# Decoding float64 weights: signs moved to GpSimd, and a third raw buffer

## The chip, the cores and the metric

The program runs on one core of one Trainium2 chip. The metric is the device time of one execution in microseconds (us), from runs on the chip; the median of the runs stands for a kernel. The hardware profiler takes one execution apart: TensorE matmuls (PE), TensorE weight loads (PEld), VectorE (DVE), ScalarE (ACT), GpSimd (POOL) and the DMA queue of SyncE (SP). About 0.2% (1.4 us) is what a measurement of this kernel can tell from no change.

## The reference

The reference is an attention layer followed by a gated feed-forward layer. Attention has 4 batches, 8 heads, 768 positions and a head width of 64; a position sees the first 8 keys and the 95 keys before itself, with a penalty that grows with distance. The feed-forward layer takes 3072 tokens of width 512 through 2048 hidden units:

```python
x = attn_out.transpose(0, 2, 1, 3).reshape(B * S, H * D)
h = x @ w_in
g = h * np.clip(h + 3.0, 0.0, 6.0) / 6.0
return (g @ w_out).astype(np.float32)
```

The two weight matrices are float64 (random numbers divided by the square root of 512 or of 2048), everything else is float32. Nothing on the chip computes in float64 here, so the kernel reads each weight as two 32-bit words and builds a float32 from them.

## The kernel before, in words

**Tiling.** The 3072 tokens form 8 blocks of 384 (`TB`). The hidden width is cut into 16 slices of 128 (index f). For each block and slice TensorE makes `hp = w1[f]^T x` (12 matmuls on line 166), ScalarE and VectorE gate it (lines 177 and 178) and split the result into a high part `gh` (line 184 or 186) and a rest `gl` (line 191), and 9 more matmuls (line 198) add it to the block's output. Each float32 operand is kept as two parts, hi and lo, and three products stand for one.

**Attention** works on pairs of heads, 4 pairs for a block, so pairs 0 to 11 belong to the first three blocks, which are done at the start with nothing else to fill TensorE. For a pair: scores on TensorE (line 816), distances and row minimum on VectorE (line 831), exponentials on ScalarE (line 835), row sums and their reciprocal on VectorE (lines 845, 846; tile `sums`), normalization on GpSimd (line 855, six instructions, tile `n`), transposes on TensorE (lines 863 and 865, tile `tp` or `hp`, copied out on line 867), and the product with the values (line 907, tile `xp`), which goes to the block's `xh` and `xl` (lines 152 and 153).

**Weights.** They come in 32 chunks of 128 x 512 float64; chunk 2f is slice f of w_in, chunk 2f+1 slice f of w_out. Slice f can be used only when its chunks are decoded. Function `fetch` reads a chunk into a raw tile `wst` (line 363). `magnitude` takes the absolute value of the high words on ScalarE (line 371, tile `wz`) and the scaled low words on GpSimd (line 375, tile `we`). For the first 12 chunks (`helped`) GpSimd also clamps `wz` to the range in which the exponent can be moved over (line 378); for the other 20 VectorE does it (line 400). The generator `decode` then runs four steps for a chunk, all on VectorE: mask and shift (line 401); the rest `lo` of the chunk before (line 406); the sign put in from the raw high word (line 409); and the integer sum with the low word (line 415), after which the next chunk's `magnitude` is issued and ScalarE casts `hi` (line 419). The next-but-one chunk is fetched right behind the sign step. There are two tiles each of `wst`, `wz` and `we`.

**Order.** The instructions of TensorE, SyncE's queue and GpSimd are kept in the order in which the program issues them (`in_order`); those of VectorE and ScalarE are placed by a scheduler when the program is built. Where decoding steps fall among attention and matmuls is set by `work`, which adds up stated costs of TensorE and VectorE work and issues steps (each yields its own stated cost) while VectorE's sum is the smaller, up to `allowed`; `decoded_to` issues what a slice must have before it is used. Engines run in order: an instruction that waits holds up all behind it on its engine or queue.

## Time and profile before

| what | value |
|---|---|
| median of 3 runs (lowest, highest) | 676.43 us (676.08, 676.55) |
| span of the profiled execution | 675.4 us |
| TensorE matmuls busy | 658.0 us, 97% |
| VectorE, ScalarE, GpSimd busy | 421.2, 278.5, 230.2 us |
| mean granted TensorE clock | 0.992 |
| decoding, from the first to the last instruction on `wz` | 16.6 to about 169 us |

The span runs from the first to the last instruction. A timeline row has the start, the duration, engine, line, operation, the tiles written and read, and in square brackets how long the engine was idle before it and what released it. A duration contains some 0.06 to 0.1 us in which the next instruction has already begun, so the distance between two starts is the better cost of an instruction that follows another.

### The profile page before, as it was taken

How to read it: one execution, taken by the hardware profiler on the slowest of the kernel's cores; microseconds unless marked ns; L12 is line 12 of the kernel's file. 1: busy time of each engine (PE TensorE's matmuls, PEld its weight loads, DVE VectorE, ACT ScalarE, POOL GpSimd, SP SyncE). 2: the span in 40 equal slices, each digit the busy share in tenths (PEclk: the TensorE clock that was granted, in tenths of full speed). 3: DMA queues.
4: the chain of work that ended last, by engine and by line, in shares of the span. 5: the costliest groups of instructions: out<-in, count | busy, mean ns of one | idle time of the engine just before them, and what ended most of it. 6: DMA issues, size and time to landing. Idle time of an engine off the chain costs nothing.

```text
span 675.4 us, 11454 instructions
## 1 busy us (share of the span) xinstructions
PE 658.0 (97%) x3963; PEld 587.2 (87%) x3963; DVE 421.2 (62%) x1109; ACT 278.5 (41%) x736; POOL 230.2 (34%) x401
## 2 busy tenths in 40 slices
PE   9989599999999999999999999999999999999997
PEld 7769488888999999989998999899898999989995
DVE  6798889999324776557663777547763677422222
ACT  6898555655225433143332444143331434221111
POOL 5778642221001443324341444314531444302110
PEclk9999889999999999999999999999999999999999
DMA  8675444442003267635654266734455255610001
GB/s 290 185 249 183 168 151 154 138 144 94 1 1 113 67 167 195 167 95 139 151 148 125 93 161 175 195 94 117 129 166 152 71 154 142 141 48 2 1 1 52
DMA packets 60836, 84.73 MB, mean 125 GB/s; under 512 B 8416, under 2 KB 45536, under 8 KB 60768
## 3 DMA queue, kind: packets, MB, share of 16 engines
q1 hardware_dynamic: 60480, 83.64, 42.7%
q8 instruction: 33, 0.54, 0.3%
q14 instruction: 35, 0.29, 0.1%
q10 hardware_dynamic: 288, 0.26, 0.1%
HBM read 62.92 MB, written 20.97 MB: 124 GB/s over the span
## 4 chain that ended last, share of the span: by engine, by line
PE 79%; DVE 9%; DMA 5%; ACT 3%; POOL 2%; issue 2%; SPq 0%; POOLq 0%; ACTq 0%; DVEq 0%
PE hp L166 34%; PE acc L198 32%; DMA wst<-w 5%; PE xp L907 2%; PE sp L820 2%; PE tp L907 2%; DVE wz L409 2%; PE tp L820 2%; ACT n L835 2%; DVE wz L415 1%; POOL n L855 1%; PE xp L358 1%; DVE wz L401 1%; DVE n L831 1%; DVE gl L191 1%
## 5 line engine op out<-in xcount | busy, mean ns | idle before, releaser
L177 ACT ACTIVATE g<-hp,small 128x384 f32<-128x384 f32 x127 | 73.7, 580 | 251.6 <-PE hp L166 230.5
L166 PE MATMUL hp<-xh,w1h 128*128 128x384 f32 x512 | 174.0, 340 | 0.0
L166 PE MATMUL hp<-xh,w1l 128*128 128x384 f32 x512 | 172.7, 337 | 0.0
L166 PE MATMUL hp<-xl,w1h 128*128 128x384 f32 x512 | 171.9, 336 | 0.0
L184 POOL TENSOR_SCALAR gh<-g 128x384 fp32r<-128x384 f32 x96 | 51.8, 540 | 292.3 <-DVE g L178 261.7
L198 PE MATMUL acc<-w2h,gl 128*128 128x512 f32 x336 | 133.8, 398 | 0.2
L198 PE MATMUL acc<-w2l,gh 128*128 128x512 f32 x336 | 133.1, 396 | 0.0
L198 PE MATMUL acc<-w2h,gh 128*128 128x512 f32 x336 | 132.9, 395 | 0.0
L178 DVE SCALAR_TENSOR_TENSOR g<-g,hp 128x384 f32<-128x384 f32 x128 | 69.7, 545 | 90.1 <-ACT g L177 89.7
L191 DVE TENSOR_TENSOR gl<-g,gh 128x384 fp32r<-128x384 f32 x128 | 80.6, 630 | 53.2 <-POOL gh L184 44.9
L855 POOL TENSOR_SCALAR n<-n,sums 128x232 f32<-128x232 f32 (+1 forms) x186 | 103.1, 570 | 31.2 <-DVE sums L846 17.6
L835 ACT ACTIVATE n<-n,least 128x232 f32<-128x232 f32 (+1 forms) x192 | 89.3, 468 | 44.0 <-DVE least L831 42.0
L166 PEld LDWEIGHTS hp<-xh,w1h 128*128 128x128 f32 x512 | 96.3, 188 | 5.5 <-issue 1.5
L166 PEld LDWEIGHTS hp<-xl,w1h 128*128 128x128 f32 x512 | 96.2, 188 | 3.9
L166 PEld LDWEIGHTS hp<-xh,w1l 128*128 128x128 f32 x512 | 96.0, 188 | 0.0
L198 PEld LDWEIGHTS acc<-w2h,gl 128*128 128x128 f32 x336 | 63.4, 189 | 15.4 <-DVE gl L191 1.7
L198 PEld LDWEIGHTS acc<-w2h,gh 128*128 128x128 f32 x336 | 63.8, 190 | 10.4 <-POOL gh L184 0.3
L198 PEld LDWEIGHTS acc<-w2l,gh 128*128 128x128 f32 x336 | 63.6, 189 | 10.4
L880 DVE STREAM_TRANSPOSE blocks<-n 128x256 f32<-128x256 f32 x112 | 43.5, 424 | 30.5 <-POOL n L855 17.3
L375 POOL TENSOR_SCALAR we<-wst 128x512 int32<-128x512 uint32 x32 | 26.6, 832 | 64.6 <-DMA wst<-w 56.7
L791 POOL TENSOR_SCALAR kx<-load 64x504 fp32r<-64x504 f32 (+1 forms) x40 | 31.1, 778 | 43.9 <-PE hp L166 42.3
L831 DVE CUSTOM_DVE_ANT_0 n<-sp,d 128x232 f32<-128x232 f32 (+1 forms) x70 | 23.6, 374 | 29.6 <-PE sp L820 29.1
(111 smaller groups left out, 788.3 us busy)
## 6 DMA issues: line engine op xcount, KB each, us to landing
wst<-w SPq DMA_DIRECT2D x32, 512.0 KB, 3.5
load<-pairs SPq DMA_DIRECT2D x22, 636.0 KB, 5.2
there<-blocks SPq DMA_DIRECT2D x52, 256.0 KB, 2.6
load<-pairs SPq DMA_DIRECT2D x32, 384.0 KB, 4.2
weights<-there SPq DMA_DIRECT2D x48, 192.0 KB, 3.9
out<-o SPq DMA_DIRECT2D x23, 256.0 KB, 2.1
weights<-there SPq DMA_DIRECT2D x32, 160.0 KB, 3.2
load<-pairs SPq DMA_DIRECT2D x9, 444.0 KB, 4.2
```

The lines of the kernel that those rows point to most:

```text
L166: self.nc.tensor.matmul(hp, lhsT=self.w1(w, f)[:, kt, :], rhs=a[:, kt, :], start=(n == 0), stop=(n == 3 * NKT - 1))
L177: nc.scalar.activation(out=g, in_=hp, func=AF.Relu, bias=self.three, scale=1.0)
L178: nc.vector.scalar_tensor_tensor(out=g, in0=g, scalar=6.0, in1=hp, op0=ALU.min, op1=ALU.mult)
L184: self.nc.gpsimd.tensor_scalar(out=gh, in0=g, scalar1=1.0, scalar2=0.0, op0=ALU.mult, op1=ALU.add)
L191: self.nc.vector.tensor_tensor(out=gl, in0=g, in1=gh.bitcast(F32), op=ALU.subtract)
L198: self.nc.tensor.matmul(acc[tt], lhsT=a[:, tk], rhs=self.w2(w, f), start=(f == 0 and j == 0), stop=(f == NF - 1 and j == 2))
L791: nc.gpsimd.tensor_scalar(out=part["kx"][own, c], in0=k[own, c], scalar1=1.0, scalar2=0.0, op0=ALU.mult, op1=ALU.add)
L820: nc.tensor.matmul(sp[j][:, lo:W], lhsT=q[:, t], rhs=part["kx"][:, c], start=(m == 0), stop=(m == 1))
L831: nc.vector.tensor_tensor_reduce(out=e[:, j, lo:W], in0=sp[j][:, lo:W], in1=d, op0=ALU.add, op1=ALU.min, scale=scale, scalar=3.0e38, accum ...
L835: nc.scalar.activation(out=e[:, j, lo:W], in_=e[:, j, lo:W], func=AF.Exp, bias=self.least[:, i:i + 1], scale=-1.0, accum_out=self.sums[:, ...
L855: nc.gpsimd.tensor_scalar(out=e[:, j, lo:W], in0=e[:, j, lo:W], scalar1=over, scalar2=0.0, op0=ALU.mult, op1=ALU.add)
L880: nc.vector.transpose(out=blocks[:, :, s].rearrange("p b j q -> p j b q"), in_=e[:, :, c:c + P].rearrange("p j (b q) -> p j b q", b=4))
```

## The change

It removes the sign step on VectorE, so a chunk takes three steps. ScalarE's absolute value now has a scale of 2^-80, VectorE clamps every chunk to limits that are smaller by the same factor, and mask and shift keep one bit more. Behind the low words, GpSimd compares the raw high words with zero and writes 0 or 32768 into the upper halves of the tile `we`, as 16-bit numbers at every second place; the integer sum then brings in low word and sign together. GpSimd's clamp for the first 12 chunks is gone. The raw tiles are three, and chunk i+2 is fetched at the start of chunk i's steps. The stated costs and the limits on steps are those of three steps.

```diff
+WORDS = 3
+DOWN = 2.0 ** -80
@@ magnitude
-        self.nc.scalar.activation(out=self.z[i].bitcast(F32), in_=words[:, :, 1].bitcast(F32), func=AF.Abs)
+        high = words[:, :, 1].bitcast(F32)
+        self.nc.scalar.activation(out=self.z[i].bitcast(F32), in_=high, func=AF.Abs, scale=DOWN)
...
         self.nc.gpsimd.tensor_scalar(out=self.e[i], in0=words[:, :, 0].bitcast(U32), scalar1=2.0 ** -29, scalar2=0.0, op0=ALU.mult, op1=ALU.add)
-        if self.helped(i):
-            z = self.z[i].bitcast(F32)
-            self.nc.gpsimd.tensor_scalar(out=z, in0=z, scalar1=MOST, scalar2=LEAST, op0=ALU.min, op1=ALU.max)
+        signs = self.e[i].bitcast(U16).rearrange("p (c w) -> p c w", w=2)[:, :, 1]
+        self.nc.gpsimd.tensor_scalar(out=signs, in0=high, scalar1=0.0, scalar2=float(1 << 15), op0=ALU.is_lt, op1=ALU.mult)
@@ decode
             if a:
+                if i + 2 < N:
+                    self.fetch(i + 2)
                 z = self.z[i]
-                if not self.helped(i):
-                    ts(out=z.bitcast(F32), in0=z.bitcast(F32), scalar1=LEAST, scalar2=MOST, op0=ALU.max, op1=ALU.min)
-                ts(out=z, in0=z, scalar1=0x07FFFFFF, scalar2=3, op0=ALU.bitwise_and, op1=ALU.logical_shift_left)
-            yield (0.34 if self.helped(i) else 0.68) * a
+                ts(out=z.bitcast(F32), in0=z.bitcast(F32), scalar1=LEAST * DOWN, scalar2=MOST * DOWN, op0=ALU.max, op1=ALU.min)
+                ts(out=z, in0=z, scalar1=0x0FFFFFFF, scalar2=3, op0=ALU.bitwise_and, op1=ALU.logical_shift_left)
+            yield 0.78 * a
...
-            yield 0.6 * b
-            if a:
-                stt(out=z, in0=self.raw[i].rearrange("p (c w) -> p c w", w=2)[:, :, 1], scalar=-0x40000000, in1=z,
-                    op0=ALU.bitwise_and, op1=ALU.bitwise_or)
-                if i + 2 < N:
-                    self.fetch(i + 2)
-            yield 0.6 * a
+            yield 0.64 * b
...
-            yield 0.69 * a
+            yield 0.66 * a
@@ banded
-            self.decoding(words, 2, 2, side="right")
+            self.decoding(words, WORDS, 2, side="right")
...
-            self.allowed = 4 * NF + 3
+            self.allowed = 3 * NF + 2
```

TensorE's order is the same before and after. Three places of the other engines differ in what matters below (line numbers of the changed kernel are some lines off: 379 is the low words, 381 the signs, 401 the clamp, 402 mask and shift, 850 the normalization, 366 the fetch).

GpSimd before, from the normalization of pair 10 (tiles `n` with `sums_871`) to that of pair 11 (`sums_1007`); `we_1121` belongs to chunk 7:

```order
L855 TENSOR_SCALAR n_961<-n_961,sums_871 128x232 x2
L375 TENSOR_SCALAR we_1121<-wst_1039 128x512
L378 TENSOR_SCALAR wz_1120<-wz_1120 128x512
L375 TENSOR_SCALAR we_1153<-wst_1080 128x512
L378 TENSOR_SCALAR wz_1152<-wz_1152 128x512
L375 TENSOR_SCALAR we_1186<-wst_1134 128x512
L378 TENSOR_SCALAR wz_1185<-wz_1185 128x512
L855 TENSOR_SCALAR n_1009<-n_1009,sums_1007 128x128 x2
```

And of the change, from the normalization of pair 9 (`sums_795`) to that of pair 10 (`sums_878`); `we_1002` belongs to chunk 5:

```order
L850 TENSOR_SCALAR n_806<-n_806,sums_795 128x232 x2
L379 TENSOR_SCALAR we_1002<-wst_910 128x512
L381 TENSOR_SCALAR we_1002<-wst_910 128x512
L379 TENSOR_SCALAR we_1043<-wst_953 128x512
L381 TENSOR_SCALAR we_1043<-wst_953 128x512
L379 TENSOR_SCALAR we_1084<-wst_1007 128x512
L381 TENSOR_SCALAR we_1084<-wst_1007 128x512
L850 TENSOR_SCALAR n_880<-n_880,sums_878 128x128 x2
```

Three chunks in a row stand ahead of pair 11 before, and ahead of pair 10 now, with two (chunks 8 and 9) ahead of pair 11. Up to pair 11 the count is the same: chunks 0 to 9, two GpSimd instructions each. From chunk 12 on there is one instruction more for a chunk than before.

SyncE's queue before, around the fetches of chunks 6 to 10 (with what each waits for; names with DMAHW are earlier transfers):

```order
L363 DMA wst_998<-w 128x1024 [waits DVE_49,DMAHW5_49,Activation_49,Pool_49]
L363 DMA wst_1039<-w 128x1024 [waits DMAHW2_49,DVE_49,DMAHW6_49,Activation_49,Pool_49]
L290 DMA load2_167<-pairs 128x768 [waits DMAHW3_49,PE_49]
L363 DMA wst_1080<-w 128x1024 [waits DMAHW1_49,DVE_49,DMAHW4_49,Activation_49,Pool_49]
L363 DMA wst_1134<-w 128x1024 [waits DVE_49,DMAHW2_49,Activation_49,Pool_49]
L363 DMA wst_1168<-w 128x1024 [waits DVE_49,DMAHW4_49,Activation_49,Pool_49]
```

And of the change, around the fetches of chunks 6 to 10:

```order
L366 DMA wst_953<-w 128x1024 [waits Activation_49,Pool_49]
L293 DMA load1_73<-pairs 128x1272 [waits DMAHW1_49,PE_49]
L366 DMA wst_1007<-w 128x1024 [waits DMAHW2_49,DMAHW3_49,Activation_49,Pool_49]
L366 DMA wst_1048<-w 128x1024 [waits DMAHW6_49,Activation_49,Pool_49]
L293 DMA load2_167<-pairs 128x768 [waits DMAHW4_49,PE_49]
L366 DMA wst_1110<-w 128x1024 [waits DMAHW0_49,DMAHW5_49,Activation_49,Pool_49]
L366 DMA wst_1143<-w 128x1024 [waits DMAHW2_49,Activation_49,Pool_49]
```

The fetch no longer waits for VectorE, only for ScalarE and GpSimd to have read the chunk three before. Against the loads of attention data it stands one chunk earlier: ahead of the same load (`load2`) stood chunk 7 last, and now chunk 8.

VectorE of the change, between the row sums of pair 2 (`sums_273`) and the scores of pair 3 (`n_348`); before, the three rows on `wz` in the middle were not there, and the first of their kind (chunk 0) stood ahead of the scores of pair 6:

```order
L840 TENSOR_SCALAR sums_273<-sums_273 128x6
L841 RECIPROCAL sums_273<-sums_273 128x6
L401 TENSOR_SCALAR wz_602<-wz_602 128x512
L402 TENSOR_SCALAR wz_602<-wz_602 128x512
L401 TENSOR_SCALAR wz_644<-wz_644 128x512
L826 ISA n_348,least_80<-sp_346,p0_176 128x128
```

So three VectorE passes, on chunks 0 and 1, moved ahead of those scores.

11 lines of the change are left out of this document (5 added, 6 removed).

## The prediction, made before the changed kernel was timed

> **What bounds the kernel now.** I read the busy times by stage first, then TensorE's timeline where it is not full, then the engine that it waited for.
>
> Busy time in stretches of 10 us (start:end, length, then PE, PEld, DVE, ACT, POOL with instruction counts, the granted clock, DMA share, GB/s):
>
> ```profile
> 70.00:80.00 10.00, 5.64 (x45) 4.49 (x43) 8.67 (x15) 5.20 (x11) 4.30 (x6) 0.90 0.42 120
> 80.00:90.00 10.00, 7.22 (x39) 5.46 (x40) 6.20 (x9) 4.51 (x8) 9.12 (x12) 0.59 0.36 134
> 100.00:110.00 10.00, 9.27 (x47) 8.04 (x46) 9.85 (x20) 6.15 (x11) 2.74 (x3) 1.00 0.46 156
> 190.00:200.00 10.00, 10.00 (x52) 9.14 (x51) 2.79 (x5) 2.47 (x5) 0.00 (x0) 1.00 0.00 0
> ```
>
> Once decoding is over (about 169 us) TensorE is full and the change touches nothing. What can be won or lost lies before. The one deep hole is at 70 to 90 us, with a low clock behind it; from 100 us on TensorE is nearly full, but VectorE is too. TensorE's timeline around the hole, and for the pair before:
>
> ```profile
> 68.59 0.38 PE L863 MATMUL tp<-ident,n 128*128 128x128 f32 x2
> 73.51 0.42 PE L166 MATMUL hp<-xh,w1h 128*128 128x384 f32 x1
> 75.53 0.33 PE L166 MATMUL hp<-xh,w1l 128*128 128x384 f32 x1
> 82.74 0.99 PE L863 MATMUL tp<-ident,n 128*128 128x128 f32 x2 [6.87 <-POOL n L855]
> 90.01 0.42 PE L166 MATMUL hp<-xh,w1h 128*128 128x384 f32 x1
> ```
>
> The transposes of pair 11 wait 6.87 us for GpSimd's normalization. GpSimd's timeline says why:
>
> ```profile
> 46.32 5.79 POOL L855 TENSOR_SCALAR n<-n,sums 128x232 f32<-128x232 f32 x12 [4.17 <-PE acc L816]
> 52.19 0.66 POOL L375 TENSOR_SCALAR we<-wst 128x512 int32<-128x512 uint32 x1
> 52.94 0.61 POOL L378 TENSOR_SCALAR wz<-wz 128x512 f32<-128x512 f32 x1
> 55.15 0.69 POOL L375 TENSOR_SCALAR we<-wst 128x512 int32<-128x512 uint32 x1 [1.60 <-DMA wst<-w]
> 56.85 4.88 POOL L855 TENSOR_SCALAR n<-n,sums 128x128 f32<-128x128 f32 x6
> 64.79 0.68 POOL L375 TENSOR_SCALAR we<-wst 128x512 int32<-128x512 uint32 x1 [1.28 <-DMA wst<-w]
> 66.47 4.60 POOL L855 TENSOR_SCALAR n<-n,sums 128x128 f32<-128x128 f32 x6
> 71.15 0.68 POOL L375 TENSOR_SCALAR we<-wst 128x512 int32<-128x512 uint32 x1
> 71.91 0.95 POOL L378 TENSOR_SCALAR wz<-wz 128x512 f32<-128x512 f32 x1
> 73.56 0.67 POOL L375 TENSOR_SCALAR we<-wst 128x512 int32<-128x512 uint32 x1 [0.70 <-DMA wst<-w]
> 80.18 0.64 POOL L375 TENSOR_SCALAR we<-wst 128x512 int32<-128x512 uint32 x1 [4.93 <-DMA wst<-w]
> 81.50 4.81 POOL L855 TENSOR_SCALAR n<-n,sums 128x128 f32<-128x128 f32 x6
> ```
>
> Three chunks stand ahead of pair 11's normalization, and the third had not landed. Why so late is seen in the sign step on VectorE and the chain of waits (start, length, piece):
>
> ```profile
> 73.64 1.13 DVE L409 SCALAR_TENSOR_TENSOR wz<-wst,wz 128x512 int32<-128x512 int32 x1
> 74.91 5.10 DMA wst<-w
> ```
>
> The raw tile is free only after the sign step has ended (74.77); the transfer starts 0.14 us later and takes 5.10 us. So a loop bounds this stage: sign step, fetch, GpSimd's two instructions, mask, sign step again, with two tiles in it.
>
> **The change part by part.** The sum is made against the span, 675.4 us. The median of the runs, 676.43, lies 1.0 us above it, and I add that 1.0 at the end.
>
> *Fetch earlier, three raw tiles.* Chunk i+2 is now fetched when ScalarE and GpSimd have read chunk i-1, two chunks' work ahead of its use. From 46.32 us GpSimd then has, up to pair 11's normalization, the normalizations of pairs 7 to 10 (5.79 + 4.88 + 4.60 = 15.27 us) and seven chunks (3 to 9). A chunk takes 0.75 us for the low words (52.19 to 52.94) and 0.6 to 0.95 for the second instruction, 1.6 us at most of the places: 11.2 us. That ends at 46.32 + 15.27 + 11.2 = 72.8 us, against 81.50 now; the difference is the four waits for DMA above (1.60 + 1.28 + 0.70 + 4.93 = 8.51). Two normalization instructions (a third of 4.81, 1.6 us) must be done for the first transposes: 74.4 us. TensorE comes there at 75.53 + 0.18 = 75.71. So the wait goes, if the sign instruction costs what the clamp did. What is then late next is nothing by these rows, with 1.3 us to spare. I count 7.0 us (82.74 - 75.71) and debit 0.5 for a new wait, since TensorE comes some 1 us earlier, too.
>
> *The low clock.* From the first transpose to the next slice the same instructions took 82.74 to 90.01 = 7.27 us, and 68.59 to 73.51 = 4.92 us for the pair before: 2.35 us that came with the clock of 0.59. With no long hole I take all of it back; if half the hole stays, the bound is none of it.
>
> *GpSimd's sign instruction for the clamp, first 12 chunks.* The trace of before has no compare with a 16-bit output. The nearest rows are the low words (same strided source) and the clamp (same number of elements):
>
> ```profile
> L375 POOL TENSOR_SCALAR we<-wst x32: 643/778/1142, 29.2 to 162.1; 128x512 int32<-128x512 uint32 x32
> L378 POOL TENSOR_SCALAR wz<-wz x12: 615/937/1155, 29.9 to 88.8; 128x512 f32<-128x512 f32 x12
> ```
>
> They bound it at 0.62 and 1.16 us. I take 0.8, near both medians, and so no change; at 1.16 seven chunks cost 7 x 0.36 = 2.5 us more, of which 1.3 us are spare. *The 20 further chunks* have one GpSimd instruction more. GpSimd is busy only 2 to 3 us in 10 there (2.74 in the stretch of 100 to 110), so nothing waits; gone that cover, 20 x 0.8 = 16 us.
>
> *One VectorE pass less.* Groups of instructions over 92 to 168 us (count | busy us, mean ns | idle before):
>
> ```profile
> L415 DVE CUSTOM_DVE_ANT_0 wz<-wz,we 128x1024 uint16<-128x1024 uint16 x21 | 16.6, 792 | 0.4
> L409 DVE SCALAR_TENSOR_TENSOR wz<-wst,wz 128x512 int32<-128x512 int32 x21 | 14.3, 681 | 0.0
> L400 DVE TENSOR_SCALAR wz<-wz 128x512 f32<-128x512 f32 x20 | 9.7, 484 | 0.9 <-ACT wz L371 0.7
> ```
>
> 14.3 us leave a full VectorE. What that is worth on the path is TensorE's waits for VectorE there (a timeline row, and rows of the waits from 92 to 172 us: total, times, longest):
>
> ```profile
> 107.64 0.50 PE L198 MATMUL sp<-w2h,gl 128*128 128x512 f32 x1 [0.73 <-DVE gl L191]
> PEld sp L198 <- DVE gl L191: 2.6, 5, 1.2
> PEld acc L198 <- DVE gl L191: 1.1, 2, 0.5
> ```
>
> The bounds are 0.7 (idle matmuls) and 3.7 us (idle weight loads, which run ahead). I take 1.4: the 0.73 and as much again hidden in shorter gaps. The sum on line 415 may be stretched by GpSimd's second instruction (its mean of 0.79 is above the 0.68 it takes alone); at 0.35 us for each of 20 chunks that is 7 us of VectorE's 14, so the slack stays. In the first 12 chunks a clamp of 0.41 replaces a sign step of 0.68 to 1.2; it brings GpSimd's and VectorE's work on each other's heels but takes 3 us off VectorE.
>
> *Attention up to 51 us.* The transposes of pair 7 wait, too:
>
> ```profile
> 47.10 0.33 PE L863 MATMUL tp<-ident,n 128*128 128x128 f32 x1 [0.99 <-POOL n L855]
> 44.77 0.68 DVE L406 TENSOR_TENSOR w2l<-wz,w2h 128x512 fp32r<-128x512 f32 x1
> 45.97 0.17 DVE L846 RECIPROCAL sums<-sums 128x6 f32<-128x6 f32 x1
> ```
>
> The reciprocal stood behind the sign step and this rest; now neither is ahead of it. I take 1.0 us, between 0 and 1.7. Against it stand the three passes ahead of pair 3's scores:
>
> ```profile
> 16.63 1.22 ACT L371 ACTIVATE wz<-wst 128x512 f32<-128x512 f32 x2
> 17.81 0.29 DVE L831 CUSTOM_DVE_ANT_0 n<-sp,p 128x128 f32<-128x128 f32 x1 [0.47 <-PE acc L816]
> ```
>
> The clamp of chunk 1 needs ScalarE's value at 17.85; with 0.41 for the clamp the scores start at 18.26 and not 17.81. Behind them wait ScalarE's exponentials, so the 0.45 is paid: I debit 0.5, with 0 and 0.9 (two passes) as bounds.
>
> *Sum:* -7.0 + 0.5 - 2.35 - 1.4 - 1.0 + 0.5 = -10.75, a span of 664.6 us; with the 1.0 around it, **665.7 us**. With all terms at their bad bounds short of a rival the gain is 7.0 - 1.7 + 0.7 + 0 - 0.9 = about 5, so 671; at the good ones 7.0 + 2.35 + 3.7 + 1.7 = 14.7, so 661.7.
>
> **The rivals.**
> *GpSimd becomes the bound of the stage.* For it: GpSimd's instructions grow when VectorE works beside them (0.62 to 1.16 us above), and a compare may take longer than a multiply. If the sign instruction takes 0.5 us longer, pair 11 comes 7 x 0.5 = 3.5 us later, 1.3 us are spare, and with half of the low clock back that leaves 675.4 - 10.75 + 2.2 + 1.2 = 668.0 span, **669 us**. Against it: it does the same work on the same count of elements. [...]
>
> *The fetch stays late.* SyncE's queue is in order, and loads of attention data, which wait for TensorE, stand between the fetches. If such a load held them, the hole would stay, and only the 1.4 and the 0.5 of the balance before 51 us would be won: **674.5 us**. Against it: the fetch is issued a chunk earlier relative to the same loads.
>
> *Slower.* The sign instruction is far dearer than its neighbours. Each 0.1 us costs 0.7 us at pair 11; from 0.8 + (10.75 + 1.3) / 7 = 2.5 us it decides, and at 3 us the time is 676.4 + 7 x 0.5 = **680 us**. Nothing in the profile speaks for it but that the form is absent.
>
> *More.* VectorE and GpSimd are relieved at once, and waits that the trace hides in short gaps go as well: **662.5 us**.
>
> **How the numbers follow.** Forecast 50%, GpSimd as the bound 22%, fetch late 6%, slower 8%, more 14%. Faster by over 0.2% holds in the forecast, both of its neighbours and most of the late fetch, less a few per cent for what I have not seen: 0.88; within 0.2% 0.04; slower 0.08. The range, 662.0 to 671.0, takes in forecast, the GpSimd bound and most of the last rival.
>
> **What would show it.** Right: no wait above 1.5 us of TensorE for the normalization; clock near 1.0 in every stretch up to 170 us; GpSimd's waits for the raw tiles gone from the stage up to pair 11; sign instruction at 0.6 to 1.1 us; VectorE's wait rows for `gl` below 1 us in all; decoding over before 160 us. Wrong: a sign instruction above 1.2 us, GpSimd busy without gaps from 46 to 75 us with TensorE waiting behind it, or fetches that start when a load ahead of them does.

## The result, and the profile after

The change takes 680.31 us (median of 4 runs, 679.47 to 681.33) where the kernel before takes 676.28 in runs beside it: a ratio of 1.0058, with a 95% interval of 1.0042 to 1.0074. It is slower by 4 us; 665.7 had been predicted. The profiled execution has a span of 679.5 us, 4.1 more than that of before.

Busy time in stretches of 10 us, the change (columns as in the prediction: PE, PEld, DVE, ACT, POOL, granted clock, DMA share, GB/s):

```profile
40.00:50.00 10.00, 7.24 (x56) 5.41 (x54) 9.10 (x34) 8.40 (x26) 9.74 (x14) 0.83 0.54 159
70.00:80.00 10.00, 9.28 (x65) 8.12 (x66) 9.66 (x24) 8.47 (x21) 9.75 (x10) 1.00 0.39 140
80.00:90.00 10.00, 6.13 (x27) 4.48 (x27) 6.02 (x10) 4.03 (x8) 9.67 (x11) 0.83 0.40 144
100.00:110.00 10.00, 9.86 (x49) 8.51 (x48) 9.69 (x16) 5.29 (x11) 9.52 (x7) 1.00 0.45 166
190.00:200.00 10.00, 10.00 (x52) 9.13 (x51) 2.78 (x5) 2.40 (x5) 0.00 (x0) 1.00 0.00 0
```

GpSimd, which stood at 4.30 and 2.74 of 10 in the stretches from 70 and from 100 us, is now full: 9.5 of 10 us and more. The hole is still at 80 to 90 us, with a granted clock of 0.83 in it, and there is a second one at 40 to 50 (TensorE busy for 7.24 of 10 us, 8.78 before). From 190 us on nothing differs. One row says what fills GpSimd (the sign instruction: count, shortest, median and longest in ns, first and last start, shape):

```profile
L381 POOL TENSOR_SCALAR we<-wst x32: 2097/2188/2727, 30.5 to 160.8; 128x512 uint16<-128x512 f32 x32
```

It takes 2.19 us; the prediction had 0.8. Rows of GpSimd's timeline from pair 7's normalization to pair 11's (some left out), and rows of TensorE, with the transposes that wait for it:

```profile
45.95 3.91 POOL L850 TENSOR_SCALAR n<-n,sums 128x232 f32<-128x232 f32 x6
66.62 0.76 POOL L379 TENSOR_SCALAR we<-wst 128x512 int32<-128x512 uint32 x1
67.47 2.43 POOL L381 TENSOR_SCALAR we<-wst 128x512 uint16<-128x512 f32 x1
69.98 0.65 POOL L379 TENSOR_SCALAR we<-wst 128x512 int32<-128x512 uint32 x1
70.71 2.45 POOL L381 TENSOR_SCALAR we<-wst 128x512 uint16<-128x512 f32 x1
73.11 4.27 POOL L850 TENSOR_SCALAR n<-n,sums 128x128 f32<-128x128 f32 x6
81.94 2.10 POOL L381 TENSOR_SCALAR we<-wst 128x512 uint16<-128x512 f32 x1
83.99 4.36 POOL L850 TENSOR_SCALAR n<-n,sums 128x128 f32<-128x128 f32 x6
```

```profile
44.92 2.30 PE L902 MATMUL xp<-pt,load 128*64 128x128 f32 x24 [2.71 <-issue]
78.89 0.42 PE L169 MATMUL hp<-xh,w1h 128*128 128x384 f32 x1
84.42 0.33 PE L858 MATMUL tp<-ident,n 128*128 128x128 f32 x1 [3.16 <-POOL n L850]
91.44 0.42 PE L169 MATMUL hp<-xh,w1h 128*128 128x384 f32 x1
```

GpSimd's waits for raw tiles are gone, as predicted, but from 27.0 to 117.7 us it has no gap above 0.1 us, and pair 11's normalization starts at 83.99 instead of 81.50. Pair 7's normalization is not late: it starts at 45.95, before at 46.32. From there GpSimd has the four normalizations of pairs 7 to 10, 15.9 us in all, and seven chunks at 3.17 us each where the prediction had 1.6.

To see where the 4.1 us arise I compare the start of each slice's first matmul (line 169; 166 before) with the same start before. In this count a slice is one block's pass over one index f, numbered from 0 to 127 in the order in which TensorE does them. Slice 3 starts at 78.89 (73.51 before): 5.4 us late. Slice 4 starts at 91.44 (90.01): 1.4 late. So the change is 5.4 us late at slice 3, makes up 4.0 of them up to slice 4, and loses 2.7 again up to slice 24; behind it the difference stays constant (within 0.3 us in all rows below, 0.7 in e2_cheap). The 4.0 us are no work saved: the transposes of pair 11 start at 84.42, 1.7 us later than before. TensorE came to them later and so waited 3.16 us there instead of 6.87. So the columns of slice 3 and slice 4 aren't independent: where pair 11 waits for GpSimd, a delay ahead of slice 3 is swallowed by that wait.

All experiments are read by this measure (us against the kernel before, each from TensorE's timeline of one profiled execution, minus is earlier; the medians are of 4 to 12 runs). The kernel before has spans of 672.6 to 677.1 us in 77 executions that were timed beside the experiments, with a median of 674.2, and the one profiled here has 675.4. So what every row is compared with is some 1.2 us slow, the other end is one execution as well, and a difference of about 1 us between two rows says little:

| run | slice 0 | slice 3 | slice 4 | slice 24 | median us |
|---|---|---|---|---|---|
| the change | +3.0 | +5.4 | +1.4 | +4.1 | 680.31 |
| e1_rooms | +0.4 | +0.1 | -3.3 | -3.8 | 672.95 |
| e2_cheap | +2.7 | +5.5 | -3.1 | +6.4 | 683.33 |
| e4_two_rooms | +3.3 | +6.5 | +0.7 | +3.1 | 681.33 |
| g6_pace_dear | +3.4 | +6.5 | +1.0 | +3.1 | 678.47 |
| g3_pace_bf | +2.7 | +5.6 | -2.8 | +0.2 | 677.31 |
| g4_both | +4.5 | +7.6 | -0.2 | -0.3 | 677.79 |
| g5_both_dear | +7.8 | +13.9 | +9.6 | +8.4 | 685.82 |
| h1_late | +0.7 | +0.4 | -1.7 | -1.8 | 674.12 |
| h2_without | +1.3 | +2.1 | -5.0 | -3.4 | 672.59 |
| h3_late_lead | +1.4 | +3.6 | -4.8 | -4.4 | 673.19 |
| h4_behind | -0.6 | +1.4 | -7.6 | -2.0 | 674.56 |
| h6_lag | -0.6 | +1.4 | -7.6 | -2.4 | 674.36 |
| h7_vector_late | -1.1 | +1.0 | -8.0 | -7.9 | 669.56 |

The median of the kernel before was 675.78 to 676.28 us in the runs beside these.

### The profile page after: what moved, and what is told of

Read it like the earlier page. It is cut to its first block, busy times and chain, and to the rows that moved or that the text cites. A ratio compares the mean times of both kernels' runs of the same rounds, so it can differ in the third digit from the quotient of the medians.

```text
span 679.5 us, 11395 instructions
## 1 busy us (share of the span) xinstructions
PE 659.5 (97%) x3963; PEld 587.2 (86%) x3963; DVE 417.2 (61%) x1089; ACT 278.6 (41%) x736; POOL 291.1 (43%) x421
## 4 chain that ended last, share of the span: by engine, by line
PE 79%; DVE 8%; POOL 6%; issue 4%; ACT 1%; DMA 1%; POOLq 0%; DVEq 0%
PE hp L169 34%; PE acc L201 32%; POOL n L850 4%; PE xp L902 3%; PE sp L815 2%; PE tp L902 2%; PE tp L815 2%; DVE wz L410 2%; DVE wz L402 2%; DVE gl L194 1%; DVE wz L401 1%; POOL we L379 1%; POOL we L381 1%; PE tp L201 1%; PE xp L201 1%
## 5 line engine op out<-in xcount | busy, mean ns | idle before, releaser
L850 POOL TENSOR_SCALAR n<-n,sums 128x232 f32<-128x232 f32 (+1 forms) x186 | 104.6, 578 | 25.7 <-DVE sums L841 16.8
L381 POOL TENSOR_SCALAR we<-wst 128x512 uint16<-128x512 f32 x32 | 73.0, 2280 | 2.7
```

Of the source, the lines that this page charges most:

```text
L381: self.nc.gpsimd.tensor_scalar(out=signs, in0=high, scalar1=0.0, scalar2=float(1 << 15), op0=ALU.is_lt, op1=ALU.mult)
L850: nc.gpsimd.tensor_scalar(out=e[:, j, lo:W], in0=e[:, j, lo:W], scalar1=over, scalar2=0.0, op0=ALU.mult, op1=ALU.add)
```

## The experiments

**1. The rooms alone.** The kernel before, with three raw tiles and the early fetch; the sign step stays on VectorE.

```diff
+                if i + 2 < N:
+                    self.fetch(i + 2)
...
-                if i + 2 < N:
-                    self.fetch(i + 2)
...
-            self.decoding(words, 2, 2, side="right")
+            self.decoding(words, 3, 2, side="right")
```

> The kernel before with one part of the change: three raw tiles and the fetch of chunk i+2 at the start of chunk i's steps. Sign step on VectorE and clamp on GpSimd stay as before. Theory A (the whole loss is the price of GpSimd's sign instruction, 2.19 us where 0.8 was assumed; the earlier fetch does what was predicted): the hole ahead of pair 11 and its low clock go, 7.0 + 2.35 us less 0.5, so about 667.5 us (665.5 to 670). Theory B (fetching earlier brings nothing, because the queue is in order or the transfers collide with the loads of attention data): 674 to 678 us. Theory C (the loss comes from VectorE's new order of decoding passes) says nothing of this run beyond what A says.

Measured: 672.95 us, ratio 0.9963 (0.9947 to 0.9978), between the ranges of the theories A and B. This part of the change is a gain, 2.8 us by the medians and 3.8 by slice 24, nearly all of it between slices 3 and 4. But the hole shrinks, it doesn't go (timeline of this kernel, a row of TensorE, then one of GpSimd):

```profile
80.58 0.99 PE L863 MATMUL tp<-ident,n 128*128 128x128 f32 x2 [4.59 <-POOL n L855]
78.60 0.76 POOL L378 TENSOR_SCALAR wz<-wz 128x512 f32<-128x512 f32 x1 [1.93 <-ACT wz L371]
```

Once the transfer is early, GpSimd's clamp waits for ScalarE's absolute value (5.2 us in three waits from 45 to 82 us), which needs one of the two `wz` tiles that VectorE frees. The transfer was the last to arrive in the loop; with it early, pair 11's transposes come only 2.2 us earlier (80.58 instead of 82.74).

**2. The sign instruction made cheap.** The change with a second writing of the low words in its place; this kernel leaves the signs out.

```diff
-        self.nc.gpsimd.tensor_scalar(out=signs, in0=high, scalar1=0.0, scalar2=float(1 << 15), op0=ALU.is_lt, op1=ALU.mult)
+        self.nc.gpsimd.tensor_scalar(out=self.e[i], in0=words[:, :, 0].bitcast(U32), scalar1=2.0 ** -29, scalar2=0.0, op0=ALU.mult, op1=ALU.add)
```

> The changed kernel with its sign instruction replaced by a second writing of the same low words (0.65 us alone); it leaves the signs of the weights out. Theory A: this is the case that the prediction was made for, so 665.7 us (663 to 668). Theory B: no better than before, 675 to 680 us. Theory C: VectorE's order is the same as in the changed kernel, so it stays at 672 to 680 us although GpSimd is light.

Measured: 683.33 us, ratio 1.0115 (1.0097 to 1.0132), slower than the change and above the range of every theory. The price is therefore not the whole cause. The table shows what it is worth and where: the hole is gone (slice 3 to 4 in 7.9 us, where it was 16.5 before and 12.6 in the change), but the loss ahead of slice 3 is the same, and behind slice 4 9.4 us are lost. One reservation: decoding is packed closer here, presumably because the scheduler, which places VectorE's instructions with its own idea of durations, now takes GpSimd for cheaper. In this kernel the last chunk is decoded beside slice 17, in the change beside 20, before beside 21. The runs that follow were made to separate the two.

The timeline of this kernel, three rows of VectorE and the row of TensorE that waits for them:

```profile
37.40 0.69 DVE L409 CUSTOM_DVE_ANT_0 wz<-wz,we 128x1024 uint16<-128x1024 uint16 x1 [0.74 <-POOL we L380]
38.01 0.18 DVE L840 RECIPROCAL sums<-sums 128x6 f32<-128x6 f32 x1
38.12 0.51 DVE L156 TENSOR_TENSOR xl<-xp,xh 128x384 fp32r<-128x384 f32 x1
38.68 0.55 PE L901 MATMUL xp<-pt,load 128*64 128x128 f32 x6 [1.72 <-DVE xl L156]
```

The integer sum waits for GpSimd's second instruction, and behind it in VectorE's queue stand a reciprocal and `xl`; TensorE waits 1.72 us for `xl` before it writes the next pair's values to `xp`.

**3. What the sign costs in other forms.** The change with six forms of GpSimd instruction in turn, one for each chunk; signs are left out.

```diff
+        less = dict(scalar1=0.0, scalar2=float(1 << 15), op0=ALU.is_lt, op1=ALU.mult)
+        plain = dict(scalar1=0.0, scalar2=1.0, op0=ALU.mult, op1=ALU.add)
+        if form == 0:
+            self.nc.gpsimd.tensor_scalar(out=halves, in0=high, **less)
+        elif form == 1:
+            self.nc.gpsimd.tensor_scalar(out=test.bitcast(F32), in0=high, **less)
+        elif form == 2:
+            self.nc.gpsimd.tensor_scalar(out=halves, in0=high, **plain)
+        elif form == 3:
+            self.nc.gpsimd.tensor_scalar(out=halves, in0=high, scalar1=0.0, scalar2=float(1 << 15), op0=ALU.mult, op1=ALU.min)
+        elif form == 4:
+            self.nc.gpsimd.tensor_scalar(out=test, in0=high, **less)
+        else:
+            self.nc.gpsimd.tensor_scalar(out=test.bitcast(U16)[:, 0:DM], in0=high, **plain)
```

> The changed kernel, with the sign instruction replaced by one of six forms by chunk number, written to a tile that nobody reads; it leaves the signs out. All read 512 strided float32 as the change does. Compare to strided 16 bit (as in the change): 2.1 to 2.7 us. If the compare is dear: compare to dense float32 and to dense int32 also about 2.1, multiply-add and multiply-min to strided 16 bit about 0.65 to 0.9. If the 16-bit output or its stride is dear: the reverse, and multiply-add to dense 16 bit tells stride from type. The time of this run says nothing.

Its one time, 682.4 us, says little, since six forms are mixed. The forms, in the order of the diff but for the lines' own (387 compare to 16 bits at every second place, 389 compare to float32, 391 multiply and add to 16 bits at every second place, 393 multiply and minimum, 395 compare to int32, 397 multiply and add to dense 16 bits):

```profile
L387 POOL TENSOR_SCALAR test<-wst x6: 2220/2278/2665, 30.3 to 146.7; 128x512 uint16<-128x512 f32 x6
L389 POOL TENSOR_SCALAR test<-wst x6: 2142/2148/2451, 36.4 to 150.5; 128x512 f32<-128x512 f32 x6
L391 POOL TENSOR_SCALAR test<-wst x5: 821/847/1267, 42.8 to 133.5; 128x512 uint16<-128x512 f32 x5
L393 POOL TENSOR_SCALAR test<-wst x5: 2189/2225/2318, 48.6 to 137.2; 128x512 uint16<-128x512 f32 x5
L395 POOL TENSOR_SCALAR test<-wst x5: 2162/2312/2477, 56.0 to 140.5; 128x512 int32<-128x512 f32 x5
L397 POOL TENSOR_SCALAR test<-wst x5: 712/972/1158, 62.4 to 143.7; 128x512 uint16<-128x512 f32 x5
```

In these forms the pair of operations sets the price. Type and stride of the output hardly matter (medians of 2.28, 2.15 and 2.31 us for compare and multiply, 0.85 and 0.97 for multiply and add), nor does it take a compare: multiply with minimum, of which 0.65 to 0.9 had been expected, costs 2.2 us, too, and multiply with add 0.85. Nor is it the minimum by itself: the clamp of before, minimum with maximum on a dense source, takes 0.62 to 1.16. So a sign can be had for 0.85: the high word times 0.0 plus -0.0, written as bf16, is a zero with that sign, bit for bit the 16 bits that are wanted.

**4. Two rooms.** The change with two raw tiles.

```diff
-WORDS = 3
+WORDS = 2
```

> The changed kernel with two raw tiles in place of three; the fetch stays at the start of a chunk's steps and so waits until ScalarE and GpSimd have read that chunk. Theory A: GpSimd is busy without gaps in the changed kernel, and 2.9 us of it for a chunk hide most of a transfer of 3.5 us; but the transfer now starts only after the sign instruction, so some waits come back: 681 to 688 us. Theory B: if the earlier transfers are what harms, two tiles are better: 675 to 679 us.

Measured: 681.33 us, ratio 1.009 (1.0072 to 1.0107), 1.0 us above the change, the two ranges overlapping (679.89 to 681.84 and 679.47 to 681.33). Against the kernel before, timed beside each, the third raw tile is worth 1.5 us here, about what a measurement can tell, and by slice 24 nothing. With signs on VectorE it is worth 2.8, together with the early fetch.

From here on the theories are: **A**, the price of the sign instruction alone; **P**, VectorE is handed chunks faster than it can decode them, so that what TensorE needs waits behind decoding.

**5. VectorE in the program's order (four runs).** VectorE is added to the engines that keep the program's order, with stated costs as in the change (`x_after_dve`), with measured ones (`e6_pace_dve`), these with the signed zero (`e7_both_dve`), and the rooms alone with signs on VectorE in the same pace (`e10_vector`).

```diff
-            if i.engine in (mybir.EngineType.PE, mybir.EngineType.SP, mybir.EngineType.Pool) and "Tile" not in type(i).__name__:
+            if i.engine in (mybir.EngineType.PE, mybir.EngineType.SP, mybir.EngineType.Pool, mybir.EngineType.DVE) and "Tile" not in type(i).__name__:
@@ e6_pace_dve, e7_both_dve
-            yield 0.78 * a
+            yield 1.13 * a
...
-            yield 0.64 * b
+            yield 0.99 * b
...
-            yield 0.66 * a
+            yield 0.68 * a
@@ e7_both_dve
-        signs = self.e[i].bitcast(U16).rearrange("p (c w) -> p c w", w=2)[:, :, 1]
-        self.nc.gpsimd.tensor_scalar(out=signs, in0=high, scalar1=0.0, scalar2=float(1 << 15), op0=ALU.is_lt, op1=ALU.mult)
+        signs = self.e[i].bitcast(BF16).rearrange("p (c w) -> p c w", w=2)[:, :, 1]
+        self.nc.gpsimd.tensor_scalar(out=signs, in0=high, scalar1=0.0, scalar2=-0.0, op0=ALU.mult, op1=ALU.add)
@@ e10_vector, against e1_rooms (beside the first line)
-            yield (0.34 if self.helped(i) else 0.68) * a
+            yield 0.76 * a
...
-            yield 0.6 * b
+            yield 0.66 * b
...
-            yield 0.6 * a
+            yield 0.66 * a
...
-            yield 0.69 * a
+            yield 0.72 * a
```

> The change, with VectorE held to the program's own order as TensorE, SyncE and GpSimd already are; stated costs as in the change (2.08 us a chunk), by which the last chunk is decoded beside slice 16 to 17 (in the change beside 20, before beside 21). Theory P (VectorE is given chunks faster than it can decode them, so TensorE's gates wait behind decoding): more loss than in the change, 682 to 688 us, with VectorE at 9.9 of 10 or more from 90 us to the end of decoding and TensorE waiting for gl and xl. Theory A (only the price of GpSimd's sign instruction, 2.2 us, in the attention stage): no worse than the change, 678 to 681.

> As the run before it, but with stated costs of 2.80 us a chunk, what the change's four VectorE passes and waits were measured at; the last chunk is then beside slice 23. The sign instruction stays at 2.2 us. Theory P: the loss behind slice 3 goes, that of the attention stage (+3 to +5 us by slice 3) stays: 674 to 679 us. Theory A: as the change, 679 to 681, since the price is the same.

> As the run before it, VectorE in the same order, with the sign written as a signed zero (times 0.0, plus -0.0, to bf16) in the place of compare and multiply; by the measured forms about 0.85 us in the place of 2.2. The output is that of the change. Theory P: attention stage about as in the kernel with three raw tiles and the signs on VectorE, and no loss behind it: 667 to 672 us. Theory A: the whole gain that was forecast, 664 to 668.

> The kernel before with three raw tiles and the early fetch, signs on VectorE, clamps of the first 12 chunks on GpSimd, and VectorE in the very order of the two runs before it (last chunk beside slice 23). Theory P: 670 to 674 us, within 2 us of the cheap sign on GpSimd, since the pass saved is worth only 0.2 to 0.3 us a chunk. Theory A: 671 to 674, 5 us or more above the cheap sign.

Measured: 742.61, 740.06, 742.92 and 742.15 us. All four expectations failed: the program's own order is bad for VectorE in the whole kernel (of some 65 us more in the span 47 to 50 arise behind slice 26, where nothing is decoded), and each of the four is 16 to 17 us late by slice 26. These runs settle nothing on totals. One thing can be read inside them: from slice 8 to 22 the dense order loses 10.4 us (5.45 to 15.89), and the three paced ones lose -0.6, +0.3 and +1.6 (17.28 to 16.72, 16.33 to 16.63, 13.83 to 15.38), with the dear sign, the cheap one and the sign on VectorE. So in this order, where decoding is spread, the price of the sign matters little behind attention.

**6. Pace by a pin (two runs, dear and cheap sign).** The scheduler keeps its freedom; only chunks 12 to 31 are put behind the last `gl` that precedes them in the program, and their stated costs are 1.5 times as high. The last chunk is then decoded beside slice 23 in both.

```diff
@@ rest
         self.nc.vector.tensor_tensor(out=gl, in0=g, in1=gh.bitcast(F32), op=ALU.subtract)
+        self.rested = self.nc.cur_bb.bb.instructions[-1].name
...
+    def behind(self, i):
+
+        if i >= 12:
+            self.tc.add_manual_dep(self.nc.cur_bb.bb.instructions[-1], self.rested, mybir.DependencyInfo(
+                mybir.DependencyClass.NoSync, mybir.DependencyReason.DATA), reason="pace")
...
@@ decode
                 ts(out=z.bitcast(F32), in0=z.bitcast(F32), scalar1=LEAST * DOWN, scalar2=MOST * DOWN, op0=ALU.max, op1=ALU.min)
+                self.behind(i)
...
-            yield 0.78 * a
+            yield 0.78 * a * (1.5 if i >= 12 else 1)
```

(`lo` and the sum are pinned in the same way, the other two costs multiplied alike; `g3_pace_bf` has the signed zero of the runs above).

> The change, with chunks 12 to 31 decoded more slowly: their passes on VectorE are put behind the slice's gl that precedes them in the program, and their stated costs are 1.5 times as high, so the last chunk is decoded beside slice 23 (in the change beside 20). The sign instruction stays as it is (2.2 us). Theory P (behind attention, decoding is packed closer than VectorE can do it): the 2.7 us that the change loses between slices 4 and 22 go, the attention stage stays as it is: 676.5 to 679. Theory A (the price of the sign instruction alone): as the change, 680 to 681.

> As the run before it (same pace, last chunk beside slice 23), with the sign as a signed zero (times 0.0, plus -0.0, to bf16), about 0.85 us instead of 2.2. Theory P: the 9.4 us that the second writing of the low words lost behind slice 4 go, its loss in the attention stage stays: 672 to 676. Theory A: 664 to 668, as forecast. If the pace changes nothing: about 683, as with the second writing of low words.

Measured: 678.47 us (ratio 1.0033, 1.0018 to 1.0049) and 677.31 (1.0022, 1.001 to 1.0035). With the cheap sign the loss from slice 4 to 24 falls from 9.4 to 3.0 us: there P holds for the larger part, though the time stays 1.3 us above what was expected. With the dear sign it falls from 2.7 to 2.1 in these two executions; by the medians the whole run gains 1.6 us (4.0 above the kernel before, then 2.4). So the pace is between a fifth and some 60% of what the change itself loses there, and these runs don't say which. Ahead of slice 3 nothing is won, with either price.

**7. A head start (two runs).** The two runs before, with three tiles for `wz` and `we`; a chunk's part on ScalarE and GpSimd is issued one chunk earlier (the lines that start chunk 2 are left out).

```diff
-                if i + 2 < N:
-                    self.fetch(i + 2)
+                if i + 3 < N:
+                    self.fetch(i + 3)
...
-                if i + 1 < N:
-                    self.magnitude(i + 1)
+                if i == 0:
+                    self.magnitude(1)
+                elif i + 2 < N:
+                    self.magnitude(i + 2)
...
-            self.decoding(words, WORDS, 2, side="right")
+            self.decoding(words, WORDS, 3, side="right")
```

> As the run before it, and ScalarE and GpSimd start on a chunk one chunk earlier (three tiles for wz and we in the place of two, the fetch a chunk earlier). Theory W: before slice 3 the loss comes from VectorE's sum, which waits for GpSimd's second instruction of its chunk while xl and the reductions that TensorE needs stand behind it in VectorE's queue (5.1 us of waits of the sum on that instruction between 14 and 75 us where the sign was replaced by a second writing). Then the loss before slice 3 goes with the head start: 667 to 671, and these waits fall below 1 us. If W is wrong: as the run before it.

> As the run before it (same pace, same head start), with compare and multiply at 2.2 us. The difference to the run before it is the price of the instruction at the same order of VectorE behind attention. Theory W and P: GpSimd has about 2.9 us of work a chunk and is full from 35 to 85 us, so the head start is used up by slice 2 or 3: 674 to 678. If the price didn't matter: within 1 us of the run before it.

Measured: 677.79 us (ratio 1.0023, 1.0012 to 1.0034) and 685.82 (1.0144, 1.0113 to 1.0175). The head start doesn't help; slice 3 is 2.1 us later than without it with the cheap sign and 7.3 later with the dear one. VectorE's sum still waits (the run with the cheap sign, 14 to 75 us: total, times, longest):

```profile
DVE wz L422 <- POOL we L382: 3.9, 4, 1.4
```

The scheduler used the head start to put VectorE's passes a chunk earlier, too, so the sum waits as before. That is no test of theory W (the sum's wait for GpSimd). Nor does the pair give the price at equal pace. The runs are 8.0 us apart, where the pair before it is 1.2 apart, but with the dear sign GpSimd stands still for a raw tile ahead of pair 10:

```profile
75.41 0.66 POOL L380 TENSOR_SCALAR we<-wst 128x512 int32<-128x512 uint32 x1 [6.88 <-DMA wst<-w]
```

In SyncE's queue the fetch stood behind a load of attention data that waited 13.9 us for TensorE (at most 6.1 with the cheap sign). That is the prediction's rival of the late fetch, which the head start brings about here; how much of the 8.0 us is price was not measured.

**8. What is lost ahead of slice 3 (three runs).** Three raw tiles and the paced signed zero in all. `h1_late` keeps the form of before (clamp on GpSimd, sign step on VectorE) in the first 12 chunks; `h2_without` has the change's form and leaves the signs of the first 12 chunks out; `h4_behind` has the change's form, and decoding passes in attention stand behind the last `xl` ahead of them in the program.

```diff
@@ h1_late, against e1_rooms (beside the pin)
+        else:
+            signs = self.e[i].bitcast(BF16).rearrange("p (c w) -> p c w", w=2)[:, :, 1]
+            self.nc.gpsimd.tensor_scalar(out=signs, in0=words[:, :, 1].bitcast(F32), scalar1=0.0, scalar2=-0.0, op0=ALU.mult, op1=ALU.add)
...
-            if a:
+            if a and self.helped(i):
                 stt(out=z, in0=self.raw[i].rearrange("p (c w) -> p c w", w=2)[:, :, 1], scalar=-0x40000000, in1=z,
@@ h2_without
+        if i >= 12:
             self.nc.gpsimd.tensor_scalar(out=signs, in0=high, scalar1=0.0, scalar2=-0.0, op0=ALU.mult, op1=ALU.add)
@@ h4_behind
         nc.vector.tensor_tensor(out=xl[:, pair, :], in0=ps, in1=xh[:, pair, :].bitcast(F32), op=ALU.subtract)
+        self.rested = nc.cur_bb.bb.instructions[-1].name
...
-        if i >= 12:
+        if self.rested:
```

> Three raw tiles and the early fetch; chunks 0 to 11 decoded as before (clamp on GpSimd, signs by VectorE), chunks 12 to 31 as in the change with the sign as a signed zero, paced to end beside slice 23. Theory C or W (the loss before slice 3 comes from the form of the first 12 chunks): by slice 3 within 0.5 us of the kernel before, as with three raw tiles and all signs on VectorE, and nothing lost behind: 670 to 673 us. If the loss came from elsewhere (fetch, tiles): 676 to 678.

> The change with the signed zero and paced chunks, but the signs of the first 12 chunks are left out: GpSimd has one instruction for these. Theory W: VectorE's sum no longer waits for GpSimd, the loss at slice 3 falls from 5.6 to 2.5 us or less: 672 to 675. Theory C or O: it stays at 4.5 to 6, 676 to 678.

> The change with the signed zero and paced chunks, and in attention, too, VectorE's decoding passes stand behind the last xl ahead of them in the program. Theory O (xl behind a waiting sum): the loss at slice 3 falls from 5.6 to 3 us or less, 672 to 675. Theory C: it stays, 676 to 678.

Measured: 674.12 us (ratio 0.9969, 0.9958 to 0.998; 670 to 673 had been expected), 672.59 (0.9945, 0.9928 to 0.9961) and 674.56 (0.9976, 0.9966 to 0.9985). At slice 3 they stand at +0.4, +2.1 and +1.4, where the run without these edits stands at +5.6. The last is the clearest: nothing is taken away, only the place of decoding in VectorE's queue moves. Its VectorE timeline at the place shown of the second experiment:

```profile
35.51 0.19 DVE L852 RECIPROCAL sums<-sums 128x6 f32<-128x6 f32 x1
35.62 0.55 DVE L156 TENSOR_TENSOR xl<-xp,xh 128x384 fp32r<-128x384 f32 x1
36.08 0.88 DVE L409 TENSOR_SCALAR wz<-wz 128x512 f32<-128x512 f32 x2
```

`xl` starts at 35.62 instead of 38.12, and no wait of the sum for GpSimd is left in attention. So the loss ahead of slice 3 is, for 4.1 of 5.6 us, `xl` and its neighbours standing behind decoding passes. How much of it is the sum's wait for GpSimd isn't separated: in h2_without, which was to take that wait away, the sums wait for the low words instead, 4.1 us in five waits from 14 to 75 us (2.6 in three in g3_pace_bf), and slice 3 is 3.5 us earlier all the same. In the change itself the sums wait 2.3 us there, and ahead of the `xl` that ends 0.1 us before the values of 44.92 us a sum that had waited 0.56, then clamp, mask and `lo` follow each other without idle time on VectorE:

```profile
41.04 0.59 DVE L401 TENSOR_SCALAR wz<-wz 128x512 f32<-128x512 f32 x1
41.66 0.56 DVE L402 TENSOR_SCALAR wz<-wz 128x512 int32<-128x512 int32 x1
42.15 0.67 DVE L407 TENSOR_TENSOR w2l<-wz,w2h 128x512 fp32r<-128x512 f32 x1
44.27 0.55 DVE L156 TENSOR_TENSOR xl<-xp,xh 128x384 fp32r<-128x384 f32 x1
```

**9. The head start where GpSimd clamps.** `h1_late` with the head start of experiment 7 (the same diff).

> As the first of these runs, with three tiles for wz and we, and ScalarE's and GpSimd's part of a chunk one chunk earlier. If the rest of the hole at pair 11 (4.6 us with three raw tiles alone) comes from GpSimd's clamp, which waits for a tile of wz that VectorE must free: 667 to 670, the wait below 1.5 us. If GpSimd's queue is only reordered (as the head start did in the run with the signed zero): 671 to 675.

Measured: 673.19 us (ratio 0.9946, 0.9929 to 0.9964). The clamp's waits for ScalarE fall from 5.2 to 0.3 us (45 to 82 us), and pair 11's transposes no longer wait, so the rest of the hole was the wait of the clamp for a `wz` tile. From slice 3 to 4 it needs 8.1 us, where e1_rooms needs 13.1 and h1_late 14.4. But 3.6 us are lost ahead of slice 3: the transposes start at 79.28, 1.3 us ahead of e1_rooms, and by the medians (672.95 there) nothing is won.

**10. What the saved pass is worth behind attention (two runs).** Both have attention as in `h4_behind`. `h7_vector_late` decodes chunks 12 to 31 as before, signs on VectorE, no pin; `h6_lag` keeps the signed zero on GpSimd and pins these chunks behind the `gl` of the slice before, since in `h4_behind` VectorE was idle ahead of `gl` for 8.9 us in 14 waits.

```diff
@@ h7_vector_late
+        if i < 12:
             self.nc.gpsimd.tensor_scalar(out=signs, in0=high, scalar1=0.0, scalar2=-0.0, op0=ALU.mult, op1=ALU.add)
...
+            if a and i >= 12:
+                stt(out=z, in0=self.raw[i].rearrange("p (c w) -> p c w", w=2)[:, :, 1], scalar=-0x40000000, in1=z,
+                    op0=ALU.bitwise_and, op1=ALU.bitwise_or)
+            yield 0.6 * (a and i >= 12)
...
-        if self.rested:
+        if self.rested and i < 12:
@@ h6_lag (in rest(), behind gl)
-        self.rested = self.nc.cur_bb.bb.instructions[-1].name
+        self.rested, self.newest = self.newest if getattr(self, "decoded", 0) > 36 else self.nc.cur_bb.bb.instructions[-1].name, self.nc.cur_bb.bb.instructions[-1].name
```

> Chunks 0 to 11 as in the run with the signed zero and decoding behind xl; chunks 12 to 31 as before, signs on VectorE, stated costs as before, no pin. Theory P (a pass taken from VectorE is worth little where GpSimd's second instruction stretches the others): attention is won (slice 4 at -7 to -8 us), and behind it nothing is lost, as with three raw tiles and all signs on VectorE (-0.5 from slice 4 to 22): 667 to 670 us. If the pass saved on VectorE is what counts there: 2 to 4 us above the other run of this pair.

> As the run with the signed zero and decoding behind xl, but behind attention a chunk's passes stand behind the gl of the slice before (not of the same slice, where VectorE sat idle for gl, 8.9 us in 14 waits on ScalarE's gh). Theory P: of the 5.5 us lost there between slices 4 and 22 half or more go: 669 to 672. If the pass saved on VectorE counts: 665 to 667, below the other run of this pair.

Measured: 669.56 us (ratio 0.9901, 0.988 to 0.9922) and 674.36 (0.9971, 0.9959 to 0.9982). `h7_vector_late` beats both kernels, the one before by 6.4 us and the change by 10.8 (these two were not timed side by side): nothing is lost behind slice 4, and the mean granted clock is 1.0. `h6_lag` fell short of both expectations. The groups of VectorE's instructions from 96 to 148 us (count | busy us, mean ns | idle before), first signs on VectorE:

```profile
L421 DVE SCALAR_TENSOR_TENSOR wz<-wst,wz 128x512 int32<-128x512 int32 x15 | 10.2, 679 | 0.0
L425 DVE CUSTOM_DVE_ANT_0 wz<-wz,we 128x1024 uint16<-128x1024 uint16 x14 | 9.5, 681 | 0.3
L412 DVE TENSOR_SCALAR wz<-wz 128x512 int32<-128x512 int32 x14 | 7.2, 517 | 0.1
L410 DVE TENSOR_SCALAR wz<-wz 128x512 f32<-128x512 f32 x14 | 5.8, 417 | 0.0
L417 DVE TENSOR_TENSOR w2l<-wz,w2h 128x512 fp32r<-128x512 f32 x8 | 5.4, 680 | 0.0
```

and signs on GpSimd:

```profile
L411 DVE TENSOR_SCALAR wz<-wz 128x512 int32<-128x512 int32 x14 | 10.6, 758 | 0.4
L420 DVE CUSTOM_DVE_ANT_0 wz<-wz,we 128x1024 uint16<-128x1024 uint16 x13 | 8.9, 683 | 0.0
L409 DVE TENSOR_SCALAR wz<-wz 128x512 f32<-128x512 f32 x13 | 7.9, 610 | 1.0 <-ACT wz L377 1.0
L416 DVE TENSOR_TENSOR w2l<-wz,w2h 128x512 fp32r<-128x512 f32 x7 | 5.8, 828 | 0.0
L416 DVE TENSOR_TENSOR w1l<-wz,w1h 128x512 fp32r<-128x512 f32 x6 | 5.6, 939 | 0.0
```

Five passes take 0.679 + 0.681 + 0.517 + 0.417 + 0.68 = 2.97 us a chunk; four beside GpSimd's second instruction take 0.758 + 0.683 + 0.610 + 0.88 (mean of the two `lo` rows) = 2.93. So four passes take as long as five: mask, clamp and `lo` stretch by what the fifth cost. `gl` goes the other way, 0.78 us in the first run and 0.55 in the second, so VectorE as a whole is relieved by some 0.2 us a chunk.

That GpSimd is what stretches them is seen when the passes of `h6_lag` from 92 to 168 us are sorted by what runs beside them. `lo` takes 0.67 to 0.69 us where no GpSimd instruction overlaps it (11 cases) and 1.19 to 1.20 where one does (8); the mask takes 0.42 (2 cases) and 0.54 to 0.89 (17).

Why `h6_lag` is 4.8 us slower and not equal isn't settled. Its `gl` waits for ScalarE's `gh` (3.9 us in this stretch), which the other's doesn't; the two also differ in pin and stated costs, and what makes ScalarE late there was not tried.

## Why the prediction was wrong

Up to slice 4 the sum had -7.0 + 0.5 - 2.35 - 1.0 + 0.5 = -9.35 us, and +1.4 came; behind it the sum had -1.4, and +2.7 came. The first failure is the price of the sign instruction, the second the worth of the pass taken from VectorE. The terms, in the prediction's order, against the change's trace:

- **The sign instruction at 0.8 us, with bounds of 0.62 and 1.16.** Wrong, and the first step that failed: 2.19 us. The bounds were taken from the nearest rows, multiply with add and minimum with maximum; the pair of operations was the one thing in which the new instruction differed, and it sets the price (experiment 3). By the prediction's own line (0.7 us for each 0.1, of which 1.3 us are spare) it puts pair 11's transposes 8.4 us behind the forecast of 75.7; they came at 84.42, 8.7 behind. GpSimd reaches pair 7 as early as before and has no gap from there on, so in the change this one term sets the start of slice 4.
- **The hole, -7.0 + 0.5 and -2.35 for the clock.** Nothing of it was won. The 4.0 us between slices 3 and 4 come from TensorE's later arrival, and of the 2.35 for the clock 0.25 came: from pair 11's first transpose to slice 4 there are 7.02 us, with a granted clock of 0.76 and another wait of 0.7 in them (7.27 at 0.62 before, 4.99 at 1.0 in h4_behind). With a cheap sign the hole is gone (slice 3 to 4 shorter by 8.6 in e2_cheap, 9.0 in h4_behind and h7_vector_late, and slice 4 8 us earlier in the last two), so the mechanism was right: the late transfer made the hole. What was missed is that where the form of before is kept the next wait, GpSimd's clamp for a `wz` tile, lets the transposes start only 2.2 us earlier (e1_rooms), and that GpSimd's 2.19 us fill the gap in the change. A small misreading, without weight: TensorE came to the transposes at 82.74 - 6.87 = 75.87, not at 75.71.
- **Attention up to 51 us, -1.0 + 0.5.** Wrong in sign: +3.0 by slice 0 and +5.4 by slice 3. The debit that was named came about as forecast (pair 3's scores start at 18.47 instead of 17.81, 0.7 us). But the prediction looked at the instructions that wait for one named pair; it didn't ask where the scheduler now puts clamp, mask and sum among `xl`, reductions and reciprocals. With the cheap sign, moving them behind `xl` alone takes 4.1 us of 5.6 back and brings slice 4 from -2.8 to -7.6 (h4_behind). This loss doesn't need the price: it is as large at 0.85 us. In the change itself the wait at pair 11 covers it, since an earlier TensorE would only wait longer for GpSimd; that is read from GpSimd's timeline, and no run has the dear sign with decoding behind `xl`.
- **One VectorE pass less, -1.4, and "the slack stays".** Wrong: +2.7 from slice 4 to 24. TensorE's waits for `gl`, which were to fall below 1 us, grew; its weight loads waited 2.6 us on one row before and now (92 to 172 us)

```profile
PEld sp L201 <- DVE gl L194: 4.1, 5, 1.2
```

  The stretching of the sum on line 415 was seen and priced at 7 us of 14; the other passes stretch as well, so that the four passes of experiment 10 take as long as five. VectorE's groups of the change from 96 to 148 us:

```profile
L410 DVE CUSTOM_DVE_ANT_0 wz<-wz,we 128x1024 uint16<-128x1024 uint16 x15 | 11.8, 786 | 0.0
L402 DVE TENSOR_SCALAR wz<-wz 128x512 int32<-128x512 int32 x15 | 9.6, 637 | 0.2
L401 DVE TENSOR_SCALAR wz<-wz 128x512 f32<-128x512 f32 x15 | 8.8, 589 | 0.7 <-ACT wz L375 0.6
L407 DVE TENSOR_TENSOR w2l<-wz,w2h 128x512 fp32r<-128x512 f32 x8 | 8.1, 1011 | 0.0
L407 DVE TENSOR_TENSOR w1l<-wz,w1h 128x512 fp32r<-128x512 f32 x7 | 5.6, 807 | 0.0
```

  That is 0.786 + 0.637 + 0.589 + 0.92 = 2.93 us a chunk, while the stated costs fell from 2.57 to 2.08. The program thus hands VectorE a chunk every 2.08 us of what it counts as free time, and the gates wait behind it. Spreading the chunks takes most of the loss away where the sign is cheap (6.4 of 9.4 us) and 0.6 to 1.6 of 2.7 where it is dear. That the rest of the 2.7 comes from the stretching is argued from these rows and not shown by a run of its own.
- **The 20 further sign instructions at nothing.** The cover that was named, GpSimd idle for 7 of 10 us, is used up: GpSimd is busy for 8.2 to 9.5 of 10 us in every stretch from 90 to 160. From 92 to 172 us no other engine has a wait for GpSimd in the trace, so what the instructions cost shows on VectorE, whose passes are longer beside them (experiment 10).
- **The rivals.** The slower one named the right place, GpSimd's time up to pair 11. But by its line an instruction of 2.19 us gives 676.4 - 7 x 0.31 = 674.2, and the time is 680.3. The 2.1 us of the clock that didn't come back, of which one rival counts half, and the 4.1 us between -1.4 and +2.7, which none has, make up the rest. "The fetch stays late" is refuted for the change, where no DMA wait is left in GpSimd's timeline. The 0.5 us in the rival of GpSimd as the bound is shown by no run; the sign instruction took 1.39 us more than the 0.8. Of the signs of being wrong two were seen, a sign instruction above 1.2 us and GpSimd busy without gaps from 46 to 75 us with TensorE waiting behind it.

The parts that were measured add up: +1.4 up to slice 4 and +2.7 behind it are +4.1, the difference of the spans.

## What to carry to other kernels

Price an instruction that the trace doesn't show from rows with the same operations, not from rows of the same size; where none exists, the bound is open above. A pass moved to GpSimd isn't saved where VectorE's other passes stretch beside it (here four took 2.93 us a chunk and five 2.97), so read the means of all of them, not of one. A shorter wait is no gain when the engine only came later: compare the time at which the awaited thing was ready. And when stated costs drive where work is placed, a change of those costs moves everything that shares the queue: look at what comes to stand ahead of the instruction that the busiest engine waits for.
